# Attention prologue: the order of the query and key spreads, the next pair's loads and the first score tiles

## The chip, the cores and the metric

The kernel runs on one NeuronCore of a Trainium2 chip. The metric is the device time of one execution in microseconds (us); the median of three runs of the kernel before is 518.95 us (518.83 to 519.52). The profile shows one execution of its own.

## The reference

Three layers follow each other. The first is clustered attention: a query sees a key only where both fall to the same of 16 centroids. Its output feeds a rational activation between two matrix products, and that feeds a soft mixture of experts.

```python
q_assign = np.argmax(np.einsum('bhsd,hcd->bhsc', q_n, c_n), axis=-1)
k_assign = np.argmax(np.einsum('bhsd,hcd->bhsc', k_n, c_n), axis=-1)
mask = q_assign[:, :, :, None] == k_assign[:, :, None, :]
scores = np.where(mask, scale * q @ k.T, -1e9)
attn = softmax(scores);  x = attn @ v                      # 2 x 8 heads, 768 x 64
g = P(x @ w_in) / Q(x @ w_in);  y = g @ w_out              # 1536 tokens, 512 -> 2048 -> 512
# soft mixture of experts: 8 experts x 4 slots, w1 and w2 per expert
```

## The kernel before

The 16 heads are worked in 8 pairs, a pair being two heads h = 0 and 1 on partitions 0 to 63 and 64 to 127. Each pair has 12 score tiles of 128 queries by 768 keys, one per head in turn. Tile u goes through these steps, a slot n of the main loop holding one step each of several tiles:

- `a1_mm` (L335, L336): four matmuls on PE into one PSUM tile `s`. L335 takes the operands `q1`, `k1` of the head, L336 takes `q2`, `k2`.
- `a1_neg` (L344): DVE scales the tile into `e` and takes the row minimum.
- `a1_exp` (L348): ACT takes the exponential of `e`.
- `turn` (L359) and `turned` (L365): PE transposes `e` into `sT`, ACT copies that into `eT`.
- `a2_av` (L372): PE multiplies by `v`.

There is one PSUM buffer for `s` (tile 1 alone uses the buffer of `sT`) and one for `sT`, so a `turn` waits for the copy of the tile before.

Ahead of its tiles a pair has to be prepared (`prep`). Raw queries and keys are loaded (`rawq`, `rawk`). `scores` (L216) multiplies both with the centroids on PE; `scaled` (L221) copies that on ACT; `scT` (L226) transposes it on PE; `best` and `first` find the nearest centroid on DVE; `ohT` and `masks` (L251, L256) turn the result into mask rows `nh`, and `mspread` (L264) sends these in eight DMAs to rows 64 to 79 of `q2` and `k2`. Beside this, queries and keys are split into a high and a low part (`qh`, `ql`, `ka`, `kb`) and *spread*, that is copied from SBUF to SBUF by DMA, into the operand tiles: `qh` and `ql` into `q1`, `qh` into `q2` (L299), `ka` twice into `k1` (L278), `kb` into `k2` (L281). For pair 0 the function `first_pair` does the same with half of the queries at first, and writes its mask rows with ACT and DVE (L165, L162) instead of DMAs.

All DMAs of this stage are issued by one queue, SP, in program order. The framework numbers DMAs over eight completion counters in turn, so an issue also waits for the landing of the eighth DMA before it.

The order of work on each engine is written out by hand: `plan` maps a slot to functions by engine class, and `run` calls them. For pair 1 the tuple `PREP1` names the slot of each step; the main loop starts at slot -2. `idle(n)` puts n matmuls on zeros on PE (L439).

Of the kernel before, what the change touches and what calls it, by code (L numbers as in the profile page):

```python
# [8 lines left out]
F32 = mybir.dt.float32  # L9
# [43 lines left out]
def tile_kernel(ctx, tc, qT, kT, v, cenT, cenP, consts, constsb, ab, w_in, w_out, phi, w1, w2, out, dbg=None):  # L53
# [3 lines left out]
    B, NPB, _, S = qT.shape  # L57
# [54 lines left out]
    NBUF = 2  # L112

    LEAD = 2
    PREP1 = (0, 0, 1, 1, 2, 3, 3, 4, 5, 6, 2, 3, 5, 7)

    OPENW = 4
    ops = [[{n: att.tile([128, S], F32R, name=f"{n}_{i}_{h}") for n in ("q1", "q2", "k1", "k2")}
# [20 lines left out]
    def first_pair(r, o, f):  # L139

        hold = f["hold"]
        w0 = slice(0, HS)
        ms = {}

        def q_split():
            qh, ql = (t_p.tile([128, S], F32R, tag=n, name=n) for n in ("qh", "ql"))
            hold["qh"], hold["ql"] = qh, ql
            ACT.copy(qh[:, w0], r["q"][:, w0])
            DVE.tensor_tensor(ql[:, w0], r["q"][:, w0], qh[:, w0].bitcast(F32), ALU.subtract)

        def rows(name, h):
            g = 2 * (name == "k") + h
            m = ms[name, h] = m_tile(BF16)
            oh = hold["eq"].rearrange("p i (c g) n -> p i c g n", c=2)
            for c in range(2):
                for i in range(3):
                    j = (3 * c + i) * 128
                    PE.transpose(m[64:80, j:j + 128], oh[:, i, c, g, :], identb)

        def q_rows(h, c):  # L160
            w = slice(c * HS, (c + 1) * HS)
            DVE.tensor_scalar(o[h]["q2"][64:80, w], ms["q", h][64:80, w], -1.0, None, ALU.add)  # L162

        def k_rows(h):
            ACT.activation(o[h]["k2"][64:80, :], ms["k", h][64:80, 0:S], AF.Copy, scale=BIG)  # L165

        def front(nxt):
            f["scores"]()
            q_split()
            f["ksplit"](0)  # L170
            f["ksplit"](1)
            for h in range(2):
                f["qspread"](h, w0)
            f["ksplit"](2)
            f["scaled"]()
            f["scT"]()
            f["best"](0)
            f["best"](1)
            for i in range(3):
                f["first"](i)  # L180
            idle(11)
            for h in range(2):
                rows("k", h)
                k_rows(h)
                rows("q", h)
                q_rows(h, 0)
            nxt[0]()
            idle(1)
            nxt[1]()

        def back(nxt):
            nxt[2]()
            idle(3)

        rest = [(0, "G", lambda: f["qsplit"](1)),
                (1, "S", lambda: f["qspreads"](slice(HS, S))),
                (1, "D", lambda: q_rows(0, 1)),
                (2, "D", lambda: q_rows(1, 1))]
        return front, back, rest

    def prep(p):

# [2 lines left out]
        o = ops[p % NBUF]  # L205
# [60 lines left out]
        def ksplit(i):  # L266
            if i == 0:
                ka, kb = tile_(t_p, "ka", [128, S], F32R), tile_(t_p, "kb", [128, S], F32R)
                POOL.tensor_scalar(ka, r["k"], 1.0, 1.0, ALU.mult, ALU.mult)
                for c in range(2):  # L270
                    w = slice(c * HS, (c + 1) * HS)
                    POOL.tensor_tensor(kb[:, w], r["k"][:, w], ka[:, w].bitcast(F32), ALU.subtract)
            elif i == 1:
                ka = hold["ka"]
                for h in range(2):
                    a = slice(64 * h, 64 * h + 64)
                    for dst in (o[h]["k1"][0:64, :], o[h]["k1"][64:128, :]):
                        SP.dma_start(dst.bitcast(F32), ka[a, :].bitcast(F32))  # L278
            else:
                for h in range(2):  # L280
                    SP.dma_start(o[h]["k2"][0:64, :].bitcast(F32), hold["kb"][64 * h:64 * h + 64, :].bitcast(F32))  # L281

        def qsplit(c, done=None):
            if "qh" not in hold:
# [8 lines left out]
            for h in range(2):  # L293
                qspread(h, w)

        def qspread(h, w):
            a, l = slice(64 * h, 64 * h + 64), slice(64 - 64 * h, 128 - 64 * h)
            for dst, src in ((o[h]["q1"][a, w], hold["qh"]), (o[h]["q1"][l, w], hold["ql"]), (o[h]["q2"][0:64, w], hold["qh"])):
                SP.dma_start(dst.bitcast(F32), src[a, w].bitcast(F32))  # L299

        if p == 0:
            return first_pair(r, o, locals())
# [134 lines left out]
    def idle(n):  # L437
        for _ in range(n):
            PE.matmul(rest_ps, zero[:, 0:128], zero, start=True, stop=True)  # L439

    def start():
        DVE.memset(zero, 0.0)
        idle(12)
        SP.dma_start(cP, cenP)
        SP.dma_start(cT, cenT)

        for n in "kq":
            raws.setdefault(0, {})[n] = raw_p.tile([128, S], F32, tag="raw" + n, name="raw" + n, bufs=2)
        for c in range(2):
            w = slice(c * HS, (c + 1) * HS)  # L450
            for n in "kq":
                SP.dma_start(raws[0][n][:, w], (kT if n == "k" else qT)[0, 0][:, w])
        SP.dma_start(cst, consts)
        SP.dma_start(cb, constsb.bitcast(BF16))
        load(1, "k")
        load(1, "q")

        x2, r, t = (pc[:, i, :] for i in range(3))
        csq = t_p.tile([128, HS], F32, tag="sc", name="csq")[:, 0:NH * D].rearrange("p (h d) -> p h d", h=NH)
        DVE.tensor_tensor(csq, cP, cP, ALU.mult)  # L460
        DVE.tensor_reduce(x2, csq, AX.X, ALU.add)
        DVE.tensor_scalar(r.bitcast(I32), x2.bitcast(I32), 1, None, ALU.logical_shift_right)
        DVE.tensor_scalar(r.bitcast(I32), r.bitcast(I32), float(0x1fbd1000), None, ALU.add)
        for _ in range(3):
            DVE.reciprocal(t, r)
            DVE.scalar_tensor_tensor(t, x2, 0.5, t, ALU.mult, ALU.mult)
            DVE.scalar_tensor_tensor(r, r, 0.5, t, ALU.mult, ALU.add)
        POOL.tensor_scalar(t, r, 1e-6, 1.0, ALU.add, ALU.mult)
        DVE.reciprocal(rn, t)
# [130 lines left out]
    def run(slot, engines):  # L600
        for eng in engines:
            for fn in plan.get(slot, {}).pop(eng, []):
                fn()
# [6 lines left out]
    manual = tc.manual_schedule(engines=engines | {mybir.EngineType.SP})  # L610
    manual.__enter__()
    start()
    front, back, rest = prep(0)
    SP.dma_start(ph, phi.rearrange("(c p) s -> p c s", p=128))
    SP.dma_start(coef, ab)
    steps = prep(1)
    early = [steps.pop(0)[2] for _ in range(3)]
    front(early)
    back(early)
    add(-LEAD + 1, rest)  # L620
    for slot, (_, eng, fn) in zip(PREP1, steps):
        plan.setdefault(slot, {}).setdefault(eng, []).append(fn)
    pend = None
    for n in range(-LEAD, NSL + 6):
        p, k = divmod(n, 12)
        run(n, ("L",))
        if n == 1:
            load_v(0)
        if n == 2:
            load(2, "k")  # L630
        if n == 3:
            load(2, "q")
        if n == 8:
            load_v(1)
        if k == 4 and n > 0 and p + 2 < NP:
            add(n, prep(p + 2))
        if k == 8 and 0 < p < NP - 1:
            load_v(p + 1)
        if n > 0 and k == 0 and p + 2 < NP and p:
            load(p + 2, "q")  # L640
        if n > 0 and k == 1 and p + 2 < NP and p:
            load(p + 2, "k")
        if n == NSL - OPENW:
            keep, w_p = open_w()
            for i in range(WAHEAD):
                w_load(i)
        g, rest = divmod(n - 6, 6)
        if 0 < g < 2 * NP and rest == 0:
            add(n, a2_x(g - 1))
        if n == NSL + 4:  # L650
            add(n, a2_x(g))
        if n == NSL - 8:
            DVE.tensor_scalar(ncoef, coef, -1.0, None, ALU.mult)
            DVE.tensor_tensor(babs, coef[:, 4:6], ncoef[:, 4:6], ALU.max)
        run(n, ("S", "D0", "D", "D1", "D2", "G0", "G"))
        if 0 <= n < NSL:
            turn(n)
        if pend is not None:
            a1_exp(pend)
            pend = None  # L660
        if 0 <= n < NSL:
            turned(n)
        run(n, "A")
        if n + LEAD < NSL:
            pend = n + LEAD
            if n > 0 or n == -LEAD:
                a1_mm(pend)
            a1_neg(pend)
            if n < 0:

                a1_mm(n + 1 + LEAD)
        run(n, "P")
        if n >= NSL:
            if n < NSL + 2:
                a2_av(g, range(3 * rest, 3 * rest + 3))
        elif g >= 0:
            done = sum(AV[6 * g:n - 6])
            a2_av(g, range(done, done + AV[n - 6]))
        run(n, "T")
        if n < 6 and n != -1:  # L680
            idle(2 if n < 0 else 3)
# [642 lines left out]
```

## Time and profile before

| | |
|---|---|
| median of three runs | 518.95 us |
| the profiled execution | 518.78 us |
| its span, first to last instruction | 517.0 us |
| PE busy | 501.1 us (97%) |
| DVE busy | 404.5 us (78%) |
| ACT busy | 362.7 us (70%) |
| granted TensorE clock, mean | 0.998 |

The span is 1.8 us shorter than the execution's own time. The attention stage fills roughly the first 275 us, the rational layer the next 185 us, the experts the rest. In the chain that ended last PE has 67%, DMA 13%, DVE 9% and ACT 5% of the span. The change touches the first 50 us only, so the rows below are read from that stretch.

### The profile page before, as it was taken

The page shows a single profiled execution, that of the slowest core. Times are in us where ns is not written, and L with a number is a line of the kernel's source. Part 1 is how long each engine was busy: PE and PEld are TensorE (multiplying, and loading weights), DVE is VectorE, ACT ScalarE, POOL GpSimd, SP SyncE. Part 2 cuts the span into 40 slices and gives each one's busy share as a digit, 9 for nine tenths or more (in the row PEclk, how much of TensorE's full clock was granted, in tenths as well). Part 3 has the DMA queues.
Part 4 walks back from the last instruction along what each step waited for, and adds up shares of the span by engine and source line. Part 5 has one row for each costly group of instructions (what it writes and reads, how often), then busy time and mean ns, then how long its engine had stood idle before and what let it go on. Part 6 is the DMA issues. An engine that isn't in the chain of part 4 may idle for free.

```text
span 517.0 us, 9835 instructions
## 1 busy us (share of the span) xinstructions
PE 501.1 (97%) x3446; PEld 336.0 (65%) x3446; DVE 404.5 (78%) x746; ACT 362.7 (70%) x646; POOL 274.3 (53%) x316
## 2 busy tenths in 40 slices
PE   8899999999999999999999999999999999999994
PEld 3556666666666666666666877777777768764362
DVE  5698899798998988988642999999799996985022
ACT  2587778888778888778772888879588786861111
POOL 4253876549686496765423856555365544551000
PEclk9999999999999999999999999999999999999999
DMA  7998989787996869873402767766466765789997
GB/s 218 249 227 223 315 244 301 223 248 218 261 298 173 285 200 287 249 216 129 160 5 61 261 226 263 278 223 234 181 228 235 266 231 178 289 325 403 422 418 307
DMA packets 44944, 126.18 MB, mean 244 GB/s; under 512 B 7136, under 2 KB 9696, under 8 KB 40288
## 3 DMA queue, kind: packets, MB, share of 16 engines
q1 hardware_dynamic: 44752, 125.31, 73.9%
q8 instruction: 27, 0.44, 0.4%
q10 hardware_dynamic: 144, 0.26, 0.1%
q14 instruction: 21, 0.17, 0.1%
HBM read 89.56 MB, written 15.73 MB: 204 GB/s over the span
## 4 chain that ended last, share of the span: by engine, by line
PE 67%; DMA 13%; DVE 9%; ACT 5%; SPq 2%; issue 1%; POOL 1%; ACTq 0%; DVEq 0%
PE h L747 9%; PE av L372 9%; PE sT L359 9%; PE h L750 9%; PE h L748 9%; DMA wt<-w 7%; PE s L335 5%; PE s L336 4%; DVE e L344 4%; PE gt L794 4%; DMA raw<-w_out 3%; ACT e L348 2%; PE l L806 2%; SPq L299 2%; ACT eT L365 2%; DMA w_in<-w 1%
## 5 line engine op out<-in xcount | busy, mean ns | idle before, releaser
L348 ACT ACTIVATE e<-e,nv 128x768 f32<-128x768 f32 x96 | 90.0, 937 | 46.7 <-DVE e L344 42.4
L344 DVE TENSOR_SCALAR_CACHE_REDUCE e<-s 128x768 f32<-128x768 f32 x96 | 91.5, 954 | 32.9 <-PE s L336 25.6
L359 PEld LDWEIGHTS sT<-cst,e 128*128 128x128 f32 x576 | 61.3, 140 | 46.6 <-ACT eT L365 24.5
L359 PE MATMUL sT<-cst,e 128*128 128x128 f32 x576 | 83.7, 281 | 2.5 <-ACT eT L365 2.0
L747 PE MATMUL h<-xh,w 128*128 128x512 f32 x192 | 80.6, 420 | 0.0
L365 ACT COPY eT<-sT 128x768 f32<-128x768 f32 x96 | 75.4, 785 | 6.0 <-PE sT L359 5.6
L372 PE MATMUL av<-eT,vt 128*64 128x384 f32 x384 | 77.2, 504 | 0.0
L764 POOL TENSOR_SCALAR q<-u,babs 128x512 f32<-128x512 f32 x47 | 36.3, 771 | 73.9 <-ACT u L762 73.9
L508 POOL TENSOR_TENSOR w<-mh,ex 128x516 f32<-128x516 f32 x32 | 41.2, 1287 | 64.5 <-DVE ex L503 44.9
L748 PE MATMUL h<-xl,w 128*128 128x512 f32 x192 | 75.3, 392 | 0.0
L335 PE MATMUL s<-k,q 128*128 128x384 f32 x192 | 73.5, 383 | 1.7 <-DVE e L344 1.5
L336 PE MATMUL s<-k,q 80*128 80x384 f32 x192 | 65.1, 339 | 1.1 <-DMA k<-kb 0.6
L766 POOL TENSOR_TENSOR q<-q,u 128x512 f32<-128x512 f32 x47 | 60.9, 1297 | 3.8
L750 PE MATMUL h<-xh,w 128*128 128x512 f32 x192 | 52.9, 396 | 0.0
L762 ACT ACTIVATE u<-h 128x512 f32<-128x512 f32 x47 | 27.9, 594 | 27.6 <-PE h L750 24.0
L747 PEld LDWEIGHTS h<-xh,w 128*128 128x128 f32 x192 | 36.1, 188 | 16.2 <-DVE r L780 4.2
L765 DVE TENSOR_TENSOR p<-p,h 128x512 f32<-128x512 f32 x47 | 32.1, 682 | 15.0 <-ACT p L763 14.9
L750 PEld LDWEIGHTS h<-xh,w 128*128 128x128 f32 x192 | 36.0, 188 | 8.6
L335 PEld LDWEIGHTS s<-k,q 128*128 128x128 f32 x192 | 36.4, 189 | 6.7 <-DVE e L344 5.9
L748 PEld LDWEIGHTS h<-xl,w 128*128 128x128 f32 x192 | 36.2, 189 | 6.7 <-issue 0.5
L772 ACT ACTIVATE r<-q,epsc 128x512 f32<-128x512 f32 x47 | 32.8, 698 | 9.2 <-POOL q L766 7.4
L336 PEld LDWEIGHTS s<-k,q 80*128 80x128 f32 x192 | 36.6, 190 | 1.8 <-issue 1.1
(198 smaller groups left out, 930.2 us busy)
## 6 DMA issues: line engine op xcount, KB each, us to landing
wt<-w SPq DMA_DIRECT2D x32, 1024.0 KB, 7.1
w<-w_in SPq DMA_DIRECT2D x96, 256.0 KB, 3.2
raw<-w_in SPq DMA_DIRECT2D x16, 512.0 KB, 5.0
raw<-w_out SPq DMA_DIRECT2D x16, 512.0 KB, 5.7
w_in<-w SPq DMA_DIRECT2D x16, 512.0 KB, 4.9
k<-ka SPq DMA_DIRECT2D x32, 192.0 KB, 5.1
q<-qh SPq DMA_DIRECT2D x28, 192.0 KB, 5.3
w_out<-w SPq DMA_DIRECT2D x16, 256.0 KB, 4.7
```

The lines of the kernel that those rows point to most:

```text
L335: PE.matmul(ps[:, c, 0:HS], o["q1"][:, it], o["k1"][:, w], start=True, stop=False)
L336: PE.matmul(ps[:, c, 0:HS], o["q2"][0:80, it], o["k2"][0:80, w], start=False, stop=True)
L344: DVE.tensor_scalar(e, s1s.pop(u)[:, :, 0:HS], -(D ** -0.5), None, ALU.mult, ALU.min, accum_out=nvs[g][:, rest:rest + 1])
L348: ACT.activation(es[u], es[u], AF.Exp, scale=-1.0, bias=nvs[g][:, rest:rest + 1], accum_out=sums[g][:, rest:rest + 1])
L359: PE.transpose(ps[:, j // 3, j % 3 * 128:(j % 3 + 1) * 128], e[:, j, :], ident)
L365: ACT.copy(dst, eTp.pop(u)[:, :, 0:HS].rearrange("p c (j t) -> p c j t", j=3))
L372: PE.matmul(av[g][64 * h:64 * h + 64, 0:HS], vs[g // 2][:, h, j, :], eTs[g][:, h, j, :], start=(j == 0), stop=(j == 5))
L508: POOL.tensor_tensor(w.rearrange("p (r n) -> p r n", r=3), hold["mh"].bitcast(F32), hold["ex"].bitcast(F32), ALU.mult)
L747: PE.matmul(h, wh[:, c, :], xh[t][:, c, :], start=(c == 0), stop=False)
L748: PE.matmul(h, wh[:, c, :], xl[t][:, c, :], start=False, stop=False)
L750: PE.matmul(h, wl[:, c, :], xh[t][:, c, :], start=False, stop=(c == NCC - 1))
L766: POOL.tensor_tensor(q, q, u, ALU.mult)
```

## The change

On SP, pair 0's six query spreads are issued ahead of its four `ka` and two `kb` spreads; pair 1's raw loads, which stood ahead of all of these, follow them, and so do the loads `ph` and `coef`. On PE, the first two score tiles stand ahead of pair 1's `scores`; pair 1's `scaled` and `scT` move into slot 0, and its later steps (`best` to `masks`, `mspread`) to a slot one later than before. Four idle matmuls go.

```diff
-    PREP1 = (0, 0, 1, 1, 2, 3, 3, 4, 5, 6, 2, 3, 5, 7)
+    PREP1 = (-2, 0, 0, 1, 1, 2, 1, 3, 4, 4, 5, 5, 6, 2, 3, 6, 7)
-        def front(nxt):
+        def front():
             f["scores"]()
             q_split()
             f["ksplit"](0)
-            f["ksplit"](1)
-            for h in range(2):
-                f["qspread"](h, w0)
-            f["ksplit"](2)
+            for n in ("qh", "ql"):
+                for h in range(2):
+                    f["qspread"](h, w0, n)
+            for n in ("ka", "kb"):
+                for h in range(2):
+                    f["kspread"](h, n)
             f["scaled"]()
             f["scT"]()
...
                 q_rows(h, 0)
-            nxt[0]()
-            idle(1)
-            nxt[1]()
-
-        def back(nxt):
-            nxt[2]()
-            idle(3)
...
+        def kspread(h, n):
+            src = hold[n][64 * h:64 * h + 64, :].bitcast(F32)
+            for dst in (o[h]["k1"][0:64, :], o[h]["k1"][64:128, :]) if n == "ka" else (o[h]["k2"][0:64, :],):
+                SP.dma_start(dst.bitcast(F32), src)
...
-        def qspread(h, w):
+        def qspread(h, w, names=("qh", "ql")):
             a, l = slice(64 * h, 64 * h + 64), slice(64 - 64 * h, 128 - 64 * h)
-            for dst, src in ((o[h]["q1"][a, w], hold["qh"]), (o[h]["q1"][l, w], hold["ql"]), (o[h]["q2"][0:64, w], hold["qh"])):
-                SP.dma_start(dst.bitcast(F32), src[a, w].bitcast(F32))
+            for dst, n in ((o[h]["q1"][a, w], "qh"), (o[h]["q1"][l, w], "ql"), (o[h]["q2"][0:64, w], "qh")):
+                if n in names:
+                    SP.dma_start(dst.bitcast(F32), hold[n][a, w].bitcast(F32))
...
         SP.dma_start(cst, consts)
         SP.dma_start(cb, constsb.bitcast(BF16))
-        load(1, "k")
-        load(1, "q")
...
-    front, back, rest = prep(0)
-    SP.dma_start(ph, phi.rearrange("(c p) s -> p c s", p=128))
-    SP.dma_start(coef, ab)
-    steps = prep(1)
-    early = [steps.pop(0)[2] for _ in range(3)]
-    front(early)
-    back(early)
+    front, rest = prep(0)
+    front()
+    load(1, "k")
+    load(1, "q")
     add(-LEAD + 1, rest)
-    for slot, (_, eng, fn) in zip(PREP1, steps):
+    for slot, (_, eng, fn) in zip(PREP1, prep(1)):
...
         run(n, ("L",))
+        if n == -1:
+            SP.dma_start(ph, phi.rearrange("(c p) s -> p c s", p=128))
+            SP.dma_start(coef, ab)
```

On the queue of SP, from the two loads `rawk` and `rawq` of pair 1 to the first weight load `w_in`, the kernel before has this order (`k_0_0` and `q_0_0` are operand tiles of pair 0, head 0, `k_0_1` and `q_0_1` of head 1):

```order
L127 DMA rawk<-kT 128x768
L127 DMA rawq<-qT 128x768
...
L278 DMA k_0_0_119<-ka 64x768 x2
L278 DMA k_0_1_123<-ka 64x768 x2
L299 DMA q_0_0_117<-qh 64x384
...
L299 DMA q_0_1_122<-qh 64x384
L281 DMA k_0_0_120<-kb 64x768
L281 DMA k_0_1_124<-kb 64x768
L486 DMA raw_140<-w_in 128x1024
```

The changed kernel has this order there:

```order
L294 DMA q_0_0_117<-qh 64x384
...
L294 DMA q_0_1_121<-ql 64x384
L275 DMA k_0_0_119<-ka 64x768 x2
L275 DMA k_0_1_123<-ka 64x768 x2
L275 DMA k_0_0_120<-kb 64x768
L275 DMA k_0_1_124<-kb 64x768
L127 DMA rawk<-kT 128x768
L127 DMA rawq<-qT 128x768
L479 DMA raw_140<-w_in 128x1024
```

The two loads of pair 1 have moved from ahead of all twelve spreads to behind the last of them, directly ahead of `w_in`; the queries moved ahead of the keys.

On PE, after the transposes of pair 0's mask rows (L158), the kernel before goes on with pair 1's `scores`, `scT` and idle matmuls, then the first score tile (`s_292`):

```order
L158 MATMUL mb<-cb,eq 16x128
L216 MATMUL mf<-rawq,cT 32x384
...
L216 MATMUL mf<-rawk,cT 32x384
L439 LDWEIGHTS zero
L439 MATMUL rest<-zero 128x512
L226 MATMUL mf<-cst,sc 128x128 x3
...
L335 MATMUL s_292<-k_0_0_119,q_0_0_117 128x384
L336 MATMUL s_292<-k_0_0_120,q_0_0_118 128x384
```

The changed kernel has the first two tiles (`s_275`, `s_284`) there, then pair 1's `scores` (L211), the third tile (`s_303`), the first `turn` (L354) and `scT` (L221):

```order
L330 MATMUL s_275<-k_0_0_119,q_0_0_117 128x384
...
L331 MATMUL s_284<-k_0_1_124,q_0_1_122 128x384
L211 MATMUL mf<-rawq,cT 32x384
...
L211 MATMUL mf<-rawk,cT 32x384
...
L330 MATMUL s_303<-k_0_0_119,q_0_0_117 128x384
...
L354 MATMUL sT<-cst,e 128x128 x6
L221 MATMUL mf<-cst,sc 128x128 x3
L434 LDWEIGHTS zero
```

`scores` of pair 1 moved from ahead of tile 0 to between tiles 1 and 2, and `scT` to behind the first `turn`.

## Rows read from the trace of the kernel before

**Rows 1.** Chain of waits, 0 to 62 us: start us, us, what
```profile
14.57 2.81 DMA k<-kb
...
17.51 0.41 PE s L336
...
30.59 9.04 DMA raw<-w_out
...
39.65 0.51 SPq L264
...
47.70 0.41 PE s L336
```

**Rows 2.** Timeline of ACT: start us, us, engine, line, operation, tiles, shapes
```profile
4.91 0.51 ACT L148 CAST qh<-rawq 128x384 fp32r<-128x384 f32 x1 [2.90 <-DMA rawq<-qT]
...
14.90 0.58 ACT L221 ACTIVATE sc<-mf,pc 128x384 f32<-128x384 f32 x1 [1.06 <-PE mf L216]
...
21.32 0.80 ACT L365 COPY eT<-sT 128x768 f32<-128x768 f32 x1
...
31.34 0.67 ACT L256 ACTIVATE nh<-mb,cst 128x384 fp32r<-128x384 bf16 x1
...
34.34 0.73 ACT L496 ACTIVATE ex<-ex,epsc 128x516 int32<-128x516 int32 x1
```

**Rows 3.** Timeline of SP's queue, the issues
```profile
7.61 2.71 SPq L278 DMA_DIRECT2D k<-ka  x4
...
14.57 1.19 SPq L281 DMA_DIRECT2D k<-kb  x2
...
32.03 0.57 SPq L264 DMA_DIRECT2D q<-nh  x1
...
32.66 0.58 SPq L264 DMA_DIRECT2D k<-nh  x1
...
40.25 0.53 SPq L520 DMA_DIRECT2D w_in<-w  x1
```

**Rows 4.** DMA issues of 13.15 to 16.1 us and 4.9 to 5.2: KB, us to landing
```profile
q<-ql SPq DMA_DIRECT2D x1, 96.0 KB, 2.4
k<-kb SPq DMA_DIRECT2D x2, 192.0 KB, 2.9
raw<-w_in SPq DMA_DIRECT2D x1, 512.0 KB, 4.7
...
rawq<-qT SPq DMA_DIRECT2D x1, 384.0 KB, 6.4
```

**Rows 5.** Windows: us, busy of PE, PEld, DVE, ACT, POOL; clock, DMA share, GB/s
```profile
10.00:12.00 2.00, 1.47 (x10) 0.58 (x9) 1.65 (x4) 0.00 (x0) 1.25 (x2) 1.00 1.02 220
...
18.00:20.00 2.00, 2.00 (x12) 1.37 (x10) 1.68 (x3) 0.68 (x1) 1.66 (x2) 1.00 0.98 297
...
54.00:56.00 2.00, 2.00 (x13) 1.18 (x14) 2.00 (x5) 1.02 (x2) 1.92 (x3) 1.00 1.04 422
```

**Rows 6.** Timeline of PE
```profile
13.89 0.51 PE L216 MATMUL mf<-rawq,cT 128*32 128x384 f32 x1 [0.20 <-ACT k L165]
...
14.68 0.39 PE L439 MATMUL rest<-zero 128*128 128x512 bf16 x1
...
18.92 0.61 PE L439 MATMUL rest<-zero 128*128 128x512 bf16 x2
...
19.34 0.44 PE L335 MATMUL s<-k,q 128*128 128x384 f32 x1
...
20.40 0.87 PE L359 MATMUL sT<-cst,e 128*128 128x128 f32 x6
...
22.17 0.87 PE L359 MATMUL sT<-cst,e 128*128 128x128 f32 x6 [0.24 <-ACT eT L365]
...
22.86 0.45 PE L335 MATMUL s<-k,q 128*128 128x384 f32 x1
```

More of the change, by code (lines that the diff above doesn't have):

```diff
@@ L198, in first_pair @@
                 (2, "D", lambda: q_rows(1, 1))]
-        return front, back, rest
+        return front, rest
     def prep(p):
@@ L272, in ksplit @@
                     POOL.tensor_tensor(kb[:, w], r["k"][:, w], ka[:, w].bitcast(F32), ALU.subtract)
[L273 to L278, printed above, removed]
             else:
                 for h in range(2):
-                    SP.dma_start(o[h]["k2"][0:64, :].bitcast(F32), hold["kb"][64 * h:64 * h + 64, :].bitcast(F32))
+                    kspread(h, "ka" if i == 1 else "kb")
+        def kspread(h, n):
+            src = hold[n][64 * h:64 * h + 64, :].bitcast(F32)
+            for dst in (o[h]["k1"][0:64, :], o[h]["k1"][64:128, :]) if n == "ka" else (o[h]["k2"][0:64, :],):
+                SP.dma_start(dst.bitcast(F32), src)
         def qsplit(c, done=None):
```

## The prediction, made before the changed kernel was run

> **What bounds the kernel now.** I read the chain of waits over the first 62 us first, then the queue of SP, the landings of its DMAs, and PE and ACT row by row. What the reader is to see in the chain: the first score tile waits for a DMA, the `kb` spread of head 0, issued at 14.57 and used at 17.51 [rows 1]. From there to 30 us the chain runs over PE, DVE and ACT, tile by tile. Then it goes through DMAs again: a weight load `w_out` issued at 30.59 takes 9.04 us, one of pair 1's mask spreads waits for it at 39.65, pair 1's query spreads come behind that on SP, and pair 1's first tile, tile 12, gets its operands at 47.70 [rows 1]. So two events set the pace here: when pair 0's tiles start, and when pair 1's spreads land. What comes after 50 us is laid out by slots, and every DMA there is issued when a buffer comes free or a slot is reached; I take it that a lateness of pair 1's first tile moves the end by as much.
>
> DMA is full in this stretch: 220 GB/s at a share of 1.02 while spreads run (10 to 12 us), 297 GB/s where mostly loads run (18 to 20 us) [rows 5]. Landings take 2.4 us for a 96 KB query spread with little ahead of it, 4.7 us for `w_in` and 6.4 us for `rawq` of pair 1 with others around them [rows 4].
>
> **The change part by part.** *Spreads of pair 0.* ACT has `qh` ready at 4.91 + 0.51 = 5.42 [rows 2], and SP has nothing else to issue by then. Six query issues at 0.65 us (0.59 for `kb`, 0.63 from one mask spread to the next, 0.68 for `ka` [rows 3]) last to 9.3, four `ka` at 2.71 / 4 = 0.68 to 12.05, two `kb` at 0.6 to 13.25. The `kb` of head 0 is thus issued 2.5 us earlier than at 14.57. It lands less early, since the transfers queue: of the 2.4 us of a 96 KB spread 0.45 is transfer at 220 GB/s, so 1.95 is fixed; the first `ka` goes out at 9.3, and five transfers of 192 KB (0.9 us each at 220 GB/s) are through at 9.3 + 1.95 + 4.45 = 15.7, the sixth at 16.6. Before, tile 0's `kb` was there at 17.5 and head 1's about 0.8 later (2.9 us after its issue [rows 4]). Tiles 0 and 1 come about 1.7 us earlier; PE is through with them at 18.92 - 1.7 = 17.2 [rows 6].
>
> The Trainium skill (DMA: Bandwidth & Descriptors, "Anatomy of one DMA") gives a fixed 2.0 us and bytes over 436 GB/s, for the gpsimd path. The fixed part agrees with the 1.95 above, the rate does not with 220 and 297 GB/s; by it `kb` would be there at 14.5 and the load below at 17.05.
>
> *Pair 1's loads.* They go out at 13.25 and 13.75, behind all spreads. Pair 1's `scores` stand on PE directly behind tile 1 and read both loads, so PE, which takes its instructions in order, stands until `rawq` is there; behind the waiting matmuls stand tile 2, the first `turn` and everything else of PE, and behind the first `turn` ACT's copy and DVE's next tile. Nothing of before shows this load in that place. Bounds: as quick as `w_in`, 13.75 + 4.7 = 18.45; as slow as this load itself was before, 13.75 + 6.4 = 20.15. Worked out: behind the last `kb` (16.6) two loads of 786 kB together at 297 GB/s, 2.65 us, so 19.3, in the middle of the two. I take 19.3.
>
> From there: `scores` 14.68 - 13.89 = 0.8, two idle matmuls 0.42, four matmuls of tile 2 at 0.2 (seven from 17.51 to 18.92 [rows 1, 6]), so the first `turn` is at 21.3 against 20.40 [rows 6]: 0.9 late in place of early.
>
> *`scT` in slot 0.* Before, `scT` was over by 16 us, under the wait for `kb`. Now it stands behind the first `turn`, and what it needs, `scaled`, stands on ACT behind the copy of that very `turn`. From the first `turn` to the second: 0.92 until ACT begins its copy, 0.80 copy, 0.58 `scaled` [rows 2], 0.1 for the two handovers, 0.43 for three transposes (half of a `turn`), three idle matmuls 0.63. That is 3.45 against 1.77 before [rows 6]: 1.7 lost, with nothing beside it, since all three engines wait on each other here. The second `turn` comes at 24.75 against 22.17, tile 3 at 25.45 against 22.86: 2.6 us late.
>
> *DVE.* `best` of pair 1 leaves slot 0 for slot 1. Both places lie under waits of DVE (tile 2's scores come late, and so do tile 3's): nothing; without that cover 1.1 us either way, within the ends above.
>
> *Pair 1's masks.* `masks` moves from slot 4 (31.34) to slot 5, where it stands behind `ex`, 34.34 + 0.73 [rows 2]: mask rows are ready at 35.74 instead of 32.01, and with the 2.6 at 38.35. Eight mask spreads at 0.63 then last to 43.4, where the store `w_in` stood at 40.25 [rows 3]: 3.15 late. The query spreads follow it as before, so tile 12 comes at 47.70 + 3.15, where by the tiles alone it would be 2.6 late; `w_out` is then issued near 33.2 and, at 9.04 us, lands by 42.3, ahead of the last mask spread. It has ceased to be what SP waits for. So 0.55 is added. Bounds of this term: 0, where the spreads land quicker on an emptier queue, and 1.2, where a mask spread waits again.
>
> *The rest.* `ph` and `coef` are read far later than they now land; four idle matmuls fewer (0.2 each) lie under PE's waits. Nothing.
>
> Sum: 2.6 + 0.55, about 3.1 us. On the profiled execution that is 518.78 + 3.1 = 521.9 (its span of 517.0 and 1.8 around it), on the median of the runs, 518.95, it is 522.0.
>
> **The rivals.** *The loads are quick.* If nothing queues ahead of them, the two are through at 13.25 + 1.95 + 786 kB at 422 GB/s, the best rate in these windows [rows 5], 1.85: 17.05. The chain then gives tile 3 at 23.2, 0.35 late, and with the mask term 0.85: 519.8, no change that can be told. For it: at 50 us loads do run at that rate. Against: the spreads ahead of them last to 16.6, and before, loads in this stretch took 4.7 and 6.4 us. This is also the time that the Trainium skill's rate would give.
>
> *The early start is kept.* If PE does not come to stand at pair 1's `scores`, the 1.7 us gained at tile 0 goes through to tile 12, less the 0.55 of the masks: 1.1 us faster, 517.85. It decides at `rawq` landing by 15.1, at which tile 3 comes 1.7 early through the same chain. For it: the first tile does get its `kb` earlier, and DVE no longer has `best` ahead of tile 2. Against: at 15.1 SP's load would be 1.35 us old.
>
> *TensorE's clock falls.* The granted clock is 1.00 in every window read [rows 5], with no wait of PE this long in them; the change has it stand some 2 us for `rawq` and 1.5 for `scaled`. If the clock falls to the lower of its two levels, 1.2 of 2.4 GHz, PE's work until tile 3 (0.8, 0.4, 0.8, 0.9, 0.4, 0.6: nearly 4 us) is doubled at the worst: 526, with 524 where half of it is hit. The Trainium skill (TensorE: Matmul & The Clock Gate, "HAM oscillation") says that waits for DMA between groups of matmuls do this; no run here shows it yet.
>
> **How the numbers follow.** Forecast 0.62, loads quick 0.20, start kept 0.10, clock 0.08. The forecast's own range: `rawq` at 18.45 and no mask term gives 1.75, at 20.15 with 1.2 it gives 4.65: 520.7 to 523.6. For 8 in 10 the quick loads have to be in: 518.6 to 523.6, which leaves out the start kept, 0.10, and the clock, 0.08. 0.2% is 1.04 us, about what a measurement of this kernel can tell from no change: faster 0.10, within 0.20, slower 0.62 + 0.08 = 0.70.
>
> **What would show it.** Right: tile 0's L331 starts near 15.7 and not 17.5; PE idle 2 us ahead of pair 1's `scores` (L211), ended by DMA `rawq`; a PE wait of about 1.4 us ahead of L221, ended by ACT; the second `turn` near 24.8; tile 12's L331 near 50.8, behind a query spread. Wrong: `rawq` landing before 17, a second `turn` at 22 or earlier, or a later stretch after 50 us that is shorter than before and so gives the time back.

## The result and the profile after

The changed kernel takes 522.11 us (median of ten runs, 520.16 to 524.19), the kernel before 518.89 us in the ten runs beside it (517.62 to 520.66). The ratio is 1.0065 with a 95% interval of 1.0048 to 1.0081: 0.65% slower, 3.4 us. The profiled execution took 521.97 us with a span of 519.9 us, 2.9 more than before; PE is busy for 500.0 us, DVE for 404.5 us, nearly as before. The mean granted clock is 0.993 instead of 0.998.

Timeline of PE in the changed kernel (start us, us, engine, line, operation, tiles, shapes, count, idle time before and what ended it); L331 is the second half of a tile's matmuls, L211 `scores`, L354 `turn`, L221 `scT`, L434 idle matmuls:

```profile
15.55 0.41 PE L331 MATMUL s<-k,q 80*128 80x384 f32 x1 [0.91 <-DMA k<-kb]
...
16.85 0.34 PE L331 MATMUL s<-k,q 80*128 80x384 f32 x1
18.37 0.82 PE L211 MATMUL mf<-rawq,cT 128*32 128x384 f32 x1 [1.18 <-DMA rawq<-qT]
...
19.81 1.04 PE L434 MATMUL rest<-zero 128*128 128x512 bf16 x2
...
21.62 0.82 PE L354 MATMUL sT<-cst,e 128*128 128x128 f32 x6
23.82 0.55 PE L221 MATMUL mf<-cst,sc 128*128 128x128 f32 x3 [1.37 <-ACT sc L216]
...
24.84 0.82 PE L354 MATMUL sT<-cst,e 128*128 128x128 f32 x6
25.42 0.42 PE L330 MATMUL s<-k,q 128*128 128x384 f32 x1
```

Tile 0 has its `kb` at 15.55 instead of 17.51 [rows 1]. PE is through with tiles 0 and 1 at 17.19 and stands until 18.37 for `rawq`. It stands once more, 1.37 us, for the scaled scores ahead of L221. From the first turn to the second it takes 24.84 - 21.62 = 3.22 us instead of 1.77, and tile 3 starts at 25.42 instead of 22.86 [rows 6]: 2.56 late. Beside that, the matmuls of L211 take 0.82 to 0.85 us here and 0.51 before [rows 6], and two idle matmuls 1.04 instead of 0.61.

The windows of that stretch say why (us; busy of PE, PEld, DVE, ACT, POOL; granted clock, DMA share, GB/s):

```profile
17.00:18.00 1.00, 0.19 (x2) 0.00 (x0) 1.00 (x3) 0.64 (x1) 0.49 (x1) 0.91 1.06 398
18.00:19.00 1.00, 0.63 (x5) 0.23 (x8) 0.76 (x3) 1.00 (x3) 0.92 (x2) 0.50 1.00 367
19.00:20.00 1.00, 1.00 (x9) 0.13 (x2) 0.00 (x0) 0.31 (x2) 1.00 (x2) 0.50 0.94 221
20.00:21.00 1.00, 1.00 (x4) 0.70 (x3) 0.00 (x0) 0.00 (x0) 0.38 (x1) 0.50 0.95 368
21.00:22.00 1.00, 1.00 (x8) 0.96 (x7) 0.18 (x1) 0.00 (x0) 0.00 (x0) 0.88 1.12 307
```

The granted clock fell to 0.50, the 1.2 GHz level, within the wait for `rawq` (0.91 in that window) and was back early in the window of 0.88, near 21.2. Before it was 1.00 at 18 to 20 us [rows 5].

SP's queue has the order that the change gives it; what answers to rows 3:

```profile
9.07 2.47 SPq L275 DMA_DIRECT2D k<-ka  x4
11.65 1.59 SPq L275 DMA_DIRECT2D k<-kb  x2
13.28 0.59 SPq L127 DMA_DIRECT2D rawk<-kT  x1
13.91 0.44 SPq L127 DMA_DIRECT2D rawq<-qT  x1
```

The landing of `rawq`, among what was issued from 13.15 to 16.1 us (KB, us to landing; rows 4 have `rawq` with 6.4):

```profile
rawq<-qT SPq DMA_DIRECT2D x1, 384.0 KB, 4.3
```

The chain of waits from 24 to 56 us (start us, us, what) still goes through pair 1's masks, and later by the route that the prediction gave:

```profile
37.43 0.66 ACT nh L251
...
43.20 0.52 SPq L513
...
46.29 3.40 DMA q<-qh
...
49.82 0.41 PE s L331
```

Mask rows are ready at 38.1, and the store behind the eight mask spreads goes out at 43.20, 2.95 later than at 40.25 [rows 3]. The query spread that tile 12's L331 waits for, the third of the six, goes out at 46.29 and lands in 3.4 us. In the kernel before it went out at 42.14 and took 5.4 (KB, us to landing):

```profile
q<-qh SPq DMA_DIRECT2D x1, 192.0 KB, 5.4
```

Tile 12 is thus only 2.12 late (49.82 against 47.70 [rows 1]). The chain of waits of the kernel before names another spread at this place, `ql` of head 1, issued at 43.93; but that one took 5.5 us and landed when tile 12 was already running.

What became of the shift can be followed over the whole run by the tile step `a1_neg` on DVE: the start of each of its 96 instances minus that of the same instance before, in us. The last two columns do the same for the start of the sixteenth and the forty-sixth `u` step of ACT in the rational layer (near 330 and 447 us).

| kernel | tile 0 | tile 3 | tile 12 | tile 24 | tile 95 | u 16th | u 46th |
|---|---|---|---|---|---|---|---|
| changed | -1.96 | +2.54 | +2.46 | +1.47 | +1.68 | +2.67 | +2.67 |
| after_again | -1.81 | +3.16 | +3.08 | +2.10 | +2.19 | +2.93 | +2.90 |
| masks_back | -1.92 | +3.12 | +3.12 | +2.12 | +2.25 | +2.26 | +2.26 |
| sct_early | -1.93 | +2.09 | +1.99 | +1.78 | +1.89 | +1.90 | +1.90 |
| fill_wait | -0.53 | +5.09 | +4.97 | +4.03 | +4.40 | +4.54 | +4.54 |
| scores_after_tile2 | -1.88 | -0.44 | -0.44 | -1.90 | -1.81 | -1.36 | -0.94 |
| no_wait | -1.77 | +0.12 | +0.02 | -0.01 | +0.18 | +0.18 | +0.19 |
| no_wait_sct_early | -1.68 | +0.65 | +0.57 | +0.07 | +0.29 | +0.74 | +0.74 |
| fill_all | -1.57 | +2.99 | +2.90 | +2.70 | +2.78 | +3.24 | +3.25 |
| loads_first_again | +1.22 | +5.19 | +5.09 | +5.01 | +5.09 | +5.10 | +5.10 |
| scores_after_turn | -1.15 | +0.04 | +1.12 | +0.21 | +0.42 | +1.02 | +0.99 |
| before_delayed | +0.16 | +2.36 | +2.35 | +0.91 | +1.03 | +1.53 | +1.53 |

### The profile page after: what moved, and what is told of

Read it like the earlier page. It is cut to its first block, busy times and chain, and to the rows that moved or that the text cites. A ratio compares the mean times of both kernels' runs of the same rounds, so it can differ in the third digit from the quotient of the medians.

```text
span 519.9 us, 9832 instructions
## 1 busy us (share of the span) xinstructions
PE 500.0 (96%) x3442; PEld 336.3 (65%) x3442; DVE 404.5 (78%) x746; ACT 362.2 (70%) x646; POOL 274.1 (53%) x316
## 4 chain that ended last, share of the span: by engine, by line
PE 63%; DVE 13%; DMA 10%; ACT 6%; issue 3%; SPq 3%; POOL 1%; DVEq 0%; ACTq 0%; POOLq 0%
PE h L740 9%; PE h L743 8%; PE h L741 8%; PE av L367 8%; PE sT L354 8%; DMA wt<-w 7%; DVE e L339 5%; PE s L330 4%; PE s L331 4%; PE gt L787 3%; ACT e L343 2%; DMA rawq<-qT 2%; ACT eT L360 2%; PE l L799 2%; SPq L259 2%
## 5 line engine op out<-in xcount | busy, mean ns | idle before, releaser
L354 PEld LDWEIGHTS sT<-cst,e 128*128 128x128 f32 x576 | 61.5, 140 | 45.7 <-ACT eT L360 24.2
L354 PE MATMUL sT<-cst,e 128*128 128x128 f32 x576 | 83.5, 281 | 2.4 <-ACT eT L360 1.9
L331 PE MATMUL s<-k,q 80*128 80x384 f32 x192 | 65.1, 339 | 1.1 <-DMA k<-kb 0.9
L740 PEld LDWEIGHTS h<-xh,w 128*128 128x128 f32 x192 | 36.1, 188 | 17.2 <-DVE r L773 5.9
L331 PEld LDWEIGHTS s<-k,q 80*128 80x128 f32 x192 | 36.7, 191 | 1.9 <-DVE q L162 1.1
```

Source lines behind the costliest of these rows:

```text
L331: PE.matmul(ps[:, c, 0:HS], o["q2"][0:80, it], o["k2"][0:80, w], start=False, stop=True)
L354: PE.transpose(ps[:, j // 3, j % 3 * 128:(j % 3 + 1) * 128], e[:, j, :], ident)
L740: PE.matmul(h, wh[:, c, :], xh[t][:, c, :], start=(c == 0), stop=False)
```

## The experiments

Each is the changed kernel with the edit shown; after_again has no edit, and the last is the kernel before. A ratio is to the kernel before on the same chip, with its 95% interval.

### no_wait: the wait taken away

Pair 1's `scores` multiply pair 0's raw queries and keys, which are long there; pair 1's masks are therefore those of pair 0. Instructions and DMAs are otherwise the same.

```diff
-    raws, vs = {}, {}
+    raws, vs, raw0 = {}, {}, {}
...
+        if p == 0:
+            raw0.update(r)
+        seen = raw0 if p == 1 else r
...
-                PE.matmul(m[32 * g:32 * g + 32, 0:HS], cT[:, hp, :], r["qk"[n]][:, c * HS:(c + 1) * HS],
+                PE.matmul(m[32 * g:32 * g + 32, 0:HS], cT[:, hp, :], seen["qk"[n]][:, c * HS:(c + 1) * HS],
```

> The changed kernel, but pair 1's scores read pair 0's raw queries and keys, which have long landed, in place of pair 1's (so the masks of pair 1 are those of pair 0; instructions and DMAs are the same). My theory (the wait for rawq and the clock's fall in it are the first term of the loss): PE goes from tile 1 straight to scores near 17.2, at a granted clock of 1.00, the first turn is near 19.2, the second 3.2 us later near 22.4, tile 3 near 23.0, that is 2.4 us ahead of the changed kernel: 519.3 to 520. Rival (the second turn is set by something else, DVE's tile 2 or ACT): tile 3 stays within 0.5 us of 25.4 and the time near 522.

Measured: 519.54 us, 1.0001 (0.9982 to 1.0021). Its timeline of PE (L214 is `scores`, L224 `scT`, L357 `turn` here):

```profile
17.26 0.51 PE L214 MATMUL mf<-rawq,cT 128*32 128x384 f32 x1
...
19.20 0.82 PE L357 MATMUL sT<-cst,e 128*128 128x128 f32 x6
21.39 0.55 PE L224 MATMUL mf<-cst,sc 128*128 128x128 f32 x3 [1.37 <-ACT sc L219]
...
22.42 0.82 PE L357 MATMUL sT<-cst,e 128*128 128x128 f32 x6
23.00 0.43 PE L333 MATMUL s<-k,q 128*128 128x384 f32 x1
```

Without the wait `scores` stand directly behind tile 1, the clock stays up (0.51 us each), and the first turn is 1.2 us earlier than before. The wait for the scaled scores takes that back: tile 3 is where it was, and the runs show no change of the time, to 0.2% either way. So no loss that the runs can tell is left without the wait for the load, the clock's fall behind it included. `scT` in its new place eats up what the early spreads gain. (The profiled execution was the longest of its twelve, 520.61 us; its span is 1.5 us longer than before, and 1.3 of that come only behind the last column of the table.)

### fill_all: the clock kept up

Idle matmuls in the three places where PE stands before `scores`: sixteen instead of eleven ahead of pair 0's masks, four ahead of tile 0, six ahead of `scores`.

```diff
-            idle(11)
+            idle(16)
...
+            idle(4)
...
+        if n == -LEAD:
+            idle(6)
```

> The changed kernel with idle matmuls in the three waits of PE from 11 to 18.4 us: five more ahead of the mask rows, four ahead of tile 0, six ahead of pair 1's scores. Theory of the clock: with PE at work in all of them the granted clock stays at 1.00 from 17 to 22 us, scores take 0.5 us a matmul, tile 3 comes about 1 us earlier than in the changed kernel, near 24.4, and the time is near 521. Rival: the clock stays up and tile 3 is at 25.4 nevertheless, since rawq and the chain over ACT set it, and the time is 522.

Measured: 520.89 us, 1.0028 (1.0005 to 1.005). Its timeline of PE (L435 idle matmuls, L212 `scores`, L355 `turn`) and two of its windows:

```profile
17.44 1.47 PE L435 MATMUL rest<-zero 128*128 128x512 bf16 x6
20.15 0.48 PE L212 MATMUL mf<-rawq,cT 128*32 128x384 f32 x1 [1.24 <-DMA rawq<-qT]
...
22.08 0.82 PE L355 MATMUL sT<-cst,e 128*128 128x128 f32 x6
...
25.88 0.42 PE L331 MATMUL s<-k,q 128*128 128x384 f32 x1
```

```profile
19.00:20.00 1.00, 0.00 (x0) 0.00 (x0) 0.19 (x1) 0.70 (x2) 0.80 (x1) 1.00 1.02 267
20.00:21.00 1.00, 0.85 (x9) 0.26 (x10) 0.00 (x0) 0.00 (x0) 0.92 (x2) 1.00 1.00 374
```

`rawq` was late in this execution, `scores` begin at 20.15, and still the clock was 1.00 throughout, though PE did nothing from 19 to 20. From `scores` to tile 3 it takes 5.73 us, against 25.42 - 18.37 = 7.05 in the changed kernel and 5.74 in no_wait: the clock's fall costs 1.3 us. This execution was the longest of its twelve (522.65 us). The intervals of the two kernels' ratios overlap a little (up to 1.005 here, from 1.0048 there), so that the filling pays in the runs is likely and not shown.

### fill_wait: the last of these fillings alone

```diff
+        if n == -LEAD:
+            idle(6)
```

> The changed kernel with six idle matmuls (1.3 us) ahead of pair 1's scores, in the time in which PE waits for rawq. Theory of the clock: the granted clock stays at 1.00 between 17 and 22 us (0.50 in the changed kernel from 18 to 21), scores take 0.5 us a matmul instead of 0.85, and tile 3 comes about 1.0 us earlier, 24.4: about 521. Rival (the clock falls by what PE did before tile 0, or the fall costs nothing since rawq and ACT set the pace): tile 3 at 25.4 as before and the time unchanged.

Measured: 520.27 us, 1.004 (1.0021 to 1.0058). The profile can't test the expectation: its execution took 523.25 us, the longest of ten, `kb` came at 16.45 in it, after 2.15 us of waiting, and the clock fell before the idle matmuls stood. The runs say a little more. Eight of the ten had a mean granted clock of 0.995 to 0.998 and took 519.80 to 520.64 us; the two with 0.990 took 522.80 and 523.25. That fits a clock that stayed up, or fell for a shorter time, in most executions of this kernel, where the ten runs of the changed kernel have 0.988 to 0.996. A mean does not say where the clock fell, and the two ratios' intervals overlap.

### sct_early: the transposes ahead of the first turn

```diff
-    PREP1 = (-2, 0, 0, 1, 1, 2, 1, 3, 4, 4, 5, 5, 6, 2, 3, 6, 7)
+    PREP1 = (-2, -1, -1, 1, 1, 2, 1, 3, 4, 4, 5, 5, 6, 2, 3, 6, 7)
```

> The changed kernel, but pair 1's scaled and scT stand in slot -1, ahead of the first turn; all else is unchanged. My theory: the wait of 1.4 us on PE ahead of scT goes, since tile 2's matmuls cover scaled; the second turn follows the first by about 1.8 us instead of 3.2; tile 3 at about 24.2 instead of 25.4, and about 1.2 us are gained, near 520.9. Rival (PE's wait for scT covers nothing but slack, since DVE's tile 2 or ACT's copy sets the pace there): tile 3 within 0.3 us of 25.4 and the time unchanged at 522.1.

Measured: 521.02 us, 1.0039 (1.0019 to 1.006). Its timeline of PE:

```profile
18.79 0.79 PE L211 MATMUL mf<-rawq,cT 128*32 128x384 f32 x1 [1.57 <-DMA rawq<-qT]
...
22.30 0.49 PE L221 MATMUL mf<-cst,sc 128*128 128x128 f32 x3
22.63 0.82 PE L354 MATMUL sT<-cst,e 128*128 128x128 f32 x6
...
24.34 0.87 PE L354 MATMUL sT<-cst,e 128*128 128x128 f32 x6 [0.24 <-ACT eT L360]
24.97 0.42 PE L330 MATMUL s<-k,q 128*128 128x384 f32 x1
```

The wait ahead of L221 is gone and the turns are 1.71 apart instead of 3.22: the 1.5 us are what `scT` costs behind the first turn. The first turn comes later, among other things by the transposes and by a `rawq` that was there only at 18.79, so that tile 3 gains only 0.45.

### no_wait_sct_early: both

The edits of no_wait and sct_early together; pair 1's masks are those of pair 0 again.

> As no_wait, and pair 1's scaled and scT stand in slot -1. My theory: both waits are gone; the second turn follows the first by 1.7 us, tile 3 near 21.8 to 22.2, 0.7 to 1 us ahead of the kernel before (22.86), and the time 517.8 to 518.7. Rival (what is gained ahead of pair 1 is taken back where its spreads or the weight loads land): tile 12 no earlier than before's, and the time as before, 518.8.

Measured: 518.57 us, 0.9994 (0.9968 to 1.002). Tile 3 was expected earlier than in the kernel before and came 0.65 later. No wait for `rawq` is left, yet the clock fell, to 0.55 at 17 to 18 us and 0.50 until 20, and `scores` took 0.85 us each again. What PE did before it fell: it stood 1.10 us for `kb` until 15.85 and was busy from then on. So the fall doesn't need the wait for the load.

### masks_back: pair 1's mask steps as early as before

```diff
-    PREP1 = (-2, 0, 0, 1, 1, 2, 1, 3, 4, 4, 5, 5, 6, 2, 3, 6, 7)
+    PREP1 = (-2, 0, 0, 1, 1, 1, 1, 2, 3, 3, 4, 5, 6, 2, 3, 5, 7)
```

> The changed kernel, but pair 1's steps from best to mspread stand one slot earlier again, masks in slot 4 and mspread in slot 5 as in the kernel before. My theory (a wait for rawq, a wait for scT behind the first turn, and masks a slot later): the first two stay, so tile 3 starts at 25.4 as in the changed kernel; mask spreads start some 3 us earlier, near 35, and tile 12's L331 comes at its tile-chain time, 49.2 to 49.5 instead of 49.8: 0.3 to 0.6 us are gained, about 521.6. Rival (what is lost by pair 1's operands is given back later anyway): no difference from the changed kernel's 522.1.

Measured: 521.14 us, 1.0052 (1.0037 to 1.0067), not to be told from the changed kernel. Tile 12 is as late as tile 3 with the masks early (3.12 and 3.12) and with the masks late (2.54 and 2.46). The later mask slot costs tile 12 nothing.

### scores_after_tile2: the scores a tile later

`scores` stand behind tile 2, `scaled` ahead of the first turn's copy on ACT, the masks in the earlier slots.

```diff
-    PREP1 = (-2, 0, 0, 1, 1, 2, 1, 3, 4, 4, 5, 5, 6, 2, 3, 6, 7)
+    PREP1 = (-1, 0, 0, 1, 1, 1, 1, 2, 3, 3, 4, 5, 6, 2, 3, 5, 7)
...
-            (2 + b, "A", scaled),
+            (2 + b, "A" if p > 1 else "A0", scaled),
...
+        run(n, ("A0",))
```

> The changed kernel's order of DMAs, but pair 1's scores stand behind tile 2, scaled ahead of the first eT copy on ACT, and masks in slot 4. My theory: if all three terms of the loss go, the 1.7 to 2.0 us gained at tile 0 is kept in good part: PE hardly waits for rawq (18.2), the first turn is near 18.9, the second near 21, tile 3 near 21.8, that is 1 us ahead of the kernel before (22.86); tile 12 about 0.7 to 1 us ahead of 47.70, and the time 518.0 to 518.4. Rival (pair 1's spreads are bound by DMA, w_out landing near 39.6 whatever the tiles do): tile 12 at 47.5 or later and the time as before, 518.9.

Measured: 518.37 us, 0.9996 (0.998 to 1.0012). Its timeline of PE:

```profile
19.13 0.51 PE L211 MATMUL mf<-rawq,cT 128*32 128x384 f32 x1 [0.70 <-DMA rawq<-qT]
...
19.91 0.88 PE L354 MATMUL sT<-cst,e 128*128 128x128 f32 x6
...
21.80 0.82 PE L354 MATMUL sT<-cst,e 128*128 128x128 f32 x6
22.38 0.42 PE L330 MATMUL s<-k,q 128*128 128x384 f32 x1
```

With tile 2 under the wait, 0.70 us of it are left, and the clock stays up. The profile shows tiles 24 to 95 some 1.8 us early and the end 1.4 (a span of 515.6 us), but the runs don't tell this kernel from the one before.

### scores_after_turn: the scores behind the first turn

As above, with `PREP1 = (0, 1, 1, 2, 2, 2, 1, 3, 4, 4, 5, 5, 6, 2, 3, 6, 7)`.

> The changed kernel with pair 1's scores on TensorE behind the first turn, the scaled copy on ACT ahead of the second turn's copy, the transposes of the scores behind tile 3, and the best-centroid step a slot later; pair 1's masks stay where the changed kernel has them. Theory: nothing between tile 0 and tile 3 waits for the load or for the scaled scores, so the 1.9 us gained at tile 0 are kept up to tile 3: first turn near 18.5, tile 3 at 20.9 to 21.6 (1.3 to 1.9 earlier than before the change), pair 1's first tile 0.5 to 1.9 earlier, time 517.0 to 518.3 us. Rival A (the load is still what PE stands for, a turn later): tile 3 at 22.5 or later, time 518.9 or more. Rival B (pair 1's first tile is bound by its spreads, not by the tiles ahead): tile 3 early but tile 12 not, time 518.6 to 519.2.

Measured: 519.1 us, 0.9996 (0.9976 to 1.0016). Its timeline of PE, and a window:

```profile
16.10 0.42 PE L331 MATMUL s<-k,q 80*128 80x384 f32 x1 [2.21 <-DMA k<-kb]
...
20.14 0.82 PE L354 MATMUL sT<-cst,e 128*128 128x128 f32 x6
20.89 0.51 PE L211 MATMUL mf<-rawq,cT 128*32 128x384 f32 x1
...
22.91 0.42 PE L330 MATMUL s<-k,q 128*128 128x384 f32 x1
```

```profile
18.00:20.00 2.00, 2.00 (x8) 1.42 (x7) 1.66 (x5) 1.57 (x3) 1.18 (x2) 0.54 1.11 371
```

No wait for `rawq` is left, but tile 3 comes at 22.91 and not at 20.9 to 21.6 as expected: `kb` was later in this execution, and behind 2.21 us of waiting for it the clock fell, so that most of tiles 0 to 2 ran at the low level and the first turn came at 20.14 instead of 18.5. What the early spreads give is lost at PE's own clock.

### loads_first and loads_first_again: the loads ahead of the spreads

```diff
         SP.dma_start(cb, constsb.bitcast(BF16))
+        load(1, "k")
+        load(1, "q")
...
     front()
-    load(1, "k")
-    load(1, "q")
```

> The changed kernel with pair 1's two raw loads issued ahead of all spreads of pair 0, as before the change; everything else of the change stays. Theory (the loss is TensorE's wait for the load, and the transposes of pair 1's score behind the first turn): the loads take their bandwidth from the spreads again, so kb is there at 17.3 to 18.2 us instead of 15.55 and tile 0 starts where it did before the change or up to 0.7 later; no wait for rawq ahead of pair 1's scores; the second turn still waits 1.4 us for the scaled scores; tile 3 is 1.2 to 2.2 us later than before the change, time 520.3 to 521.0 us. Rival A (the late loads alone are the loss): tile 3 within 0.5 us of before, time 518.9 to 519.4. Rival B (the order of queries and keys matters by itself, kb ahead of queries being no gain): tile 0 a microsecond or more later than before with time above 521.5.

> The same kernel as loads_first, one more profiled execution, since the first one took 526.28 us, 3.8 above the median of its kernel. Theory (the loads, issued first, take bandwidth from the spreads, and TensorE's longer wait for kb lets its clock fall): kb of tile 0 is used at 17.5 to 18.5 us, no wait for rawq, a wait of 1.4 us ahead of the scores' transposes, tile 3 some 2.5 to 4.5 us later than in the kernel before. Rival (the first execution was an odd one): kb used near 17.5 at a granted clock of 1.00, tile 3 1.5 us later.

Measured: 522.46 us, 1.0079 (1.0048 to 1.011); the execution of loads_first_again took 524.62 us. The timeline of PE of loads_first_again, then the issue of the `ka` spreads on SP in loads_first:

```profile
18.20 0.66 PE L331 MATMUL s<-k,q 80*128 80x384 f32 x1 [2.25 <-DMA k<-kb]
...
20.71 0.85 PE L211 MATMUL mf<-rawq,cT 128*32 128x384 f32 x1
...
26.48 0.55 PE L221 MATMUL mf<-cst,sc 128*128 128x128 f32 x3 [1.37 <-ACT sc L216]
```

```profile
10.92 3.35 SPq L275 DMA_DIRECT2D k<-ka  x4
```

`rawq` keeps nobody waiting, and the kernel is no quicker for it: `kb` is used at 18.20 (18.88 in loads_first), later than before the change. The first `ka` goes out at 10.92 instead of 9.07. The eighth DMA before it is `rawk`, issued at 4.48 and landed 6.4 us later, at 10.9. Over the wait for `kb` the clock falls too, and tile 3 is 5.2 us late (5.7 in loads_first). That the late place of the loads is by itself the loss is refuted: with the loads ahead, PE stands for `kb` instead. The size in the profiles is that of long executions (526.28 and 524.62 us, where the median is 522.46).

### after_again: the changed kernel once more

> The changed kernel once more, for a second profile. If the waits are its own and not chance: rawq lands between 18 and 19.3, the granted clock falls to 0.50 in that wait, the second turn follows the first by 3.2 us, and tile 3 is 2 to 3.5 us behind the kernel before. If the 1.0 us that the first profile lost near 328 us is chance, it is not there.

Measured: 522.15 us in one run, 520.0 span; `rawq` at 19.00, the clock at 0.50 to 0.72 from 18 to 21, turns at 22.24 and 25.46. The same picture, the load 0.6 later.

### before_delayed: the kernel before with a lateness of another cause

Twelve idle matmuls ahead of the first turn; loads, spreads and masks as before.

```diff
-        if n < 6 and n != -1:
-            idle(2 if n < 0 else 3)
+        if n < 6:
+            idle(2 if n < -1 else 12 if n < 0 else 3)
```

> The kernel before, with twelve idle matmuls on TensorE behind tile 2, ahead of the first turn, where there were none: nothing else is moved, no load, no spread, no mask step. The first turn and tile 3 come 2.2 to 2.6 us later, as in the changed kernel, by a cause that has nothing to do with loads. Theory of the prediction (a lateness at tile 3 goes through to the end whole): tile 12, tile 36 and the end are 2.2 to 2.6 us late, time 521.1 to 521.5 us. Rival (0.8 us are given back between tiles 12 and 36 whatever the cause, and what is lost again near 328 us comes from the state of the weight loads at that place): tiles 36 to 95 1.4 to 1.8 us late, time 520.3 to 520.8 us.

Measured: 520.98 us, 1.004 (1.0022 to 1.0058). Its timeline of PE:

```profile
20.30 2.77 PE L439 MATMUL rest<-zero 128*128 128x512 bf16 x12
22.91 0.82 PE L359 MATMUL sT<-cst,e 128*128 128x128 f32 x6
...
49.09 0.44 PE L335 MATMUL s<-k,q 128*128 128x384 f32 x1 [0.22 <-DVE e L344]
```

Tile 3 is 2.36 late, tile 95 only 1.03. At tile 12 the wait of PE for its spread, which the kernel before has (47.70, ended by a DMA), is gone: a late tile no longer finds its operands missing, and tile 13 is 1.61 late. By tile 24 it is 0.91; the steps in between are open. So in this execution a lateness of the prologue does not go through whole. How much of it stays, the runs tell less sharply: 0.4% is 2.1 us with an interval of 1.1 to 3.0, which does not exclude the 2.36, and the profiled execution was the quickest of its kernel.

## Why the prediction was right, and where it was not

**Early spreads: right.** `kb` was used at 15.55 (15.7 forecast), and PE was free at 17.19 (17.2).

**PE stands for `rawq`: the mechanism right, the size in the profile too large.** The forecast was 19.3 with bounds of 18.45 and 20.15. Over the executions in which `scores` waited for the load and `kb` was early, `scores` began at 18.37, 18.73, 18.79, 19.00, 19.13 and 20.15, in the profile after just below the lower bound. There `rawq` took 4.3 us instead of the 5.55 that a queue behind the last `kb` would give: from 17 to 18 us 398 GB/s were moved, not 297. no_wait shows that the loss goes when this wait goes.

**The clock's place among the rivals failed.** The clock's fall was put at 0.08, as a case of its own with 524 to 526 us, and the forecast's own sum had nothing for it. It came in the forecast's own case, in both profiles of the changed kernel, and cost 1.3 us in the first, for it was over by 21.2 and had not begun at tile 0. It hid that `rawq` had been forecast too late: 18.37 - 19.3 + 1.3 makes 0.4 us, and the first turn came 0.3 later than forecast (21.62, forecast 21.3). The Trainium skill (TensorE: Matmul & The Clock Gate, "HAM oscillation") puts such falls down to waits for DMA between groups of matmuls. The 0.50 behind the waits for `kb` and `rawq` agrees, but such waits did not always lead to a fall (1.24 us for `rawq` in fill_all). "Four idle matmuls fewer: nothing" is open. In the kernel before they stand ahead of the wait for `kb` (one at 14.68 [rows 6], three at 15.92), and the clock was 1.00 in it:

```profile
15.92 0.81 PE L439 MATMUL rest<-zero 128*128 128x512 bf16 x3
...
17.00:18.00 1.00, 0.49 (x3) 0.52 (x4) 0.00 (x0) 0.00 (x0) 0.00 (x0) 1.00 0.90 177
```

fill_all kept the clock up with fifteen more than the changed kernel has, no_wait kept it up with none more, and no run puts just these four back.

**`scT` behind the first turn: right.** 3.22 us from turn to turn (3.45 forecast), with a PE wait of 1.37 ended by ACT (1.4 forecast); sct_early takes 1.5 us of it away. Tile 3 at 25.42 (25.45 forecast) is thus right by errors that cancel.

**The mask term failed**: 0.55 forecast, nothing measured. The mask spreads ended as late as foretold (the store at 43.20, forecast 43.4), and the query spread that tile 12 waits for went out even 4.15 later than before (46.29, not 42.14). But it landed in 3.4 us instead of 5.4, and tile 12 came 2.12 late, less than tile 3: the lower bound of the term was the true one. Its reason, an emptier queue, fits: from 40 to 49 us 1.36 MB were moved, and 2.07 before.

**"A lateness moves the end by as much" failed in the profiles.** From tile 12 to tile 24 the changed kernel got back 1.0 us, before_delayed 1.4. Near 328 us it lost 1.0 again (0.7 in the second profile): PE waits 0.74 us there, and the weight load `w_out` of 1 MB took 7.4 us to land (7.2 in the second profile) instead of 5.2. Other kernels lose 0.1 to 0.6 there or 30 us earlier. Nothing is lost in masks_back, sct_early, no_wait and loads_first_again; in the first three that load took 5.3 to 5.4 us. What makes it late stays open. Without it the profile would have shown about 2 us; the forecast of 3.1 met the measured 3.4 partly by luck.

**The rivals.** *Loads quick* needed 17.05; `scores` never began before 18.37 in an execution that waited for it. *Start kept* needed 15.1. With `scores` behind tile 2 (scores_after_tile2) the early start was kept in the profile; behind the first turn (scores_after_turn) it was lost to the clock in the execution profiled. The runs of neither show a gain over the kernel before.

## What to carry to other kernels

Before a load is moved behind other transfers, look for the first instruction that reads it and for what stands behind that on the same engine: two microseconds won at the head of the queue were lost in the wait for the load, at the clock, and behind the first turn. When a change adds a wait or takes idle matmuls out of one, look at the granted clock behind it too. And test with a plain delay how much of a lateness at the front reaches the end, before adding it to a sum whole.

## What the runs showed of the hardware

- The length of one wait does not tell whether the clock falls. It fell with a wait of 1.18 us for `rawq` (the changed kernel) and with no wait for it at all (no_wait_sct_early, 1.10 us for `kb` before); it stayed at 1.00 over a wait of 1.24 us behind six idle matmuls (fill_all) and over 1.37 us ahead of `scT` (the changed kernel).
- The same load in the same place of the queue took from 4.3 us (the changed kernel) to 5.8 us (fill_all) to land, and `scores` behind it began anywhere between 18.37 and 20.15 us.
- Loads that stand first on the queue delay the spreads twice (loads_first against the changed kernel): the spreads behind them land late, the first query spread in 7.1 us instead of 2.3, and the counter that the eighth DMA before holds delays an issue, the first `ka` at 10.92 instead of 9.07.
